# Mask rows of the last batch by compute engines, a fifth head pair by the crossbar, more buffers and a new instruction order in an attention and FFN kernel

## The chip, the cores and the metric

The kernel runs on one core of one Trainium2 chip. The metric is the device time of one execution in microseconds, as the median of the runs of a kernel. The engines are called TensorE (PE in the profile; its weight loads stand apart as PEld), VectorE (DVE), ScalarE (ACT), GpSimd (POOL) and SyncE (SP). A letter q behind an engine's name (SPq) means its instruction queue issuing a DMA.

## The reference, cut to what matters

Block-sparse attention over 4 batches of 8 heads, then a feed-forward block with a gated convolution along the sequence:

```python
def _attn_ref(q, k, v, sampled_blocks):          # B, H, S, D = 4, 8, 768, 64; blocks of 32
    scores = scale * np.matmul(q, k.transpose(0, 1, 3, 2))
    mask = np.abs(blk_i - blk_j) <= 1
    mask = mask | (blk_i == 0) | (blk_j == 0) | (blk_i == n_blocks - 1) | (blk_j == n_blocks - 1)
    for qb in range(n_blocks):
        for kb in sampled_blocks[qb]:
            mask[qb * 32:(qb + 1) * 32, kb * 32:(kb + 1) * 32] = True
    scores = np.where(mask, scores, -1000000000.0)
    attn = np.exp(scores - np.max(scores, axis=-1, keepdims=True))
    return np.matmul(attn / np.sum(attn, axis=-1, keepdims=True), v)

def _moe_ref(x, w_in, conv_w, w_out):            # x: 4 x 768 x 512, d_ff 1024
    h = np.maximum(x @ w_in, 0.0)
    conv_out = sum(conv_w[k] * hp[:, k:k + S, :] for k in range(3))   # hp: h padded by one
    gate = 1.0 / (1.0 + np.exp(-conv_out))
    return h * gate @ w_out
```

## The kernel before, in words

All 16 pairs of heads (P0 to P15, four pairs to a batch) are computed densely, with the mask as extra rows of the matrix product. For each pair the kernel holds two tiles, `e` and `o`, with 88 partitions: rows 0 to 63 hold transposed K and Q, one head dimension to a row, and rows 64 to 87 hold mask rows, one for each of the 24 blocks, which add a large negative number to the scores that are masked out. There are five such slots; the mask rows of a slot are written once, and serve every pair that comes to lie in the slot. In the last batch the queries of the second half of the sequence are grouped in another way (a segment of 256 tokens and one of 128 instead of one of 384), so the mask rows for these query columns have to be replaced in the slots of P12 to P15. The new rows stand ready in the tile `mlast`; before the change eight DMAs on SP's queue, called `m_last`, bring them into the slots (line 598).

Attention runs in 144 units. A unit is a set of score matmuls into PSUM (`s`, L746, two halves of four blocks), one exp on ScalarE over 128x1024 (L757), and eight matmuls with V (`av`, L779). Units 36 to 71 belong to batch 1; its pair P4 is needed from unit 36, P5 from 40.5, P6 from 45 and P7 from 49.5 on. VectorE divides by the sum (`rcp`, `norm`, L696 and L698), and the result is transposed into `xT`, mostly by DMA transposes on SP's queue (`x_xb`, L707). Between the units the feed-forward work of the segment before is done: `f1` (L895) and a relu on ScalarE or VectorE (L915, L917), for the convolution three `mul` (L949) and two `add` (L959) on VectorE, a tanh on ScalarE (L998), `g1` and `g2` on VectorE (L1001, L1006), and then `f2` (L825) with an eviction (`ev`) and an output DMA. `f2#3` needs the gates `g2#3` of the last pair of features in its first segment.

K, Q and V are loaded by GpSimd's queue (L240), which casts them to bf16 in `nat`, `nq` and `vn`. Pairs P0 to P4 (`NPE = 5`) get K and Q transposed by TensorE (`kq_transposes`: L470 for K, L508 for Q, the second half of Q from an `nq` buffer) and copied from PSUM. Pairs from P5 on go through the crossbar (`kq_crossbar`): two DMA transposes on SP's queue from `nat` to `stg` (L585, called `xb`), and two copies of 64x1536 from `stg` to the slot (`stg_cp`), both of which need both transposes. The loads up to batch 1 are issued in the order of `SEQ`, each after the load four places ahead of it has landed (L660, `pace`); later ones wait for the exp of a given unit (L417).

The whole order is fixed beforehand. Each operation has a place in `gr.ops`; `put_down` walks the string `ORDER`, in which two letters name an operation, one more the engine where there is a choice, and one more the buffer of each allocation. Every engine then executes its own instructions strictly in that order, and so does each DMA queue issue. The costs beside each operation, such as `t_d4`, `t_act` and the `service` of a DMA, were used to make the string and have no part in the execution. At the start 44 dummy matmuls (`NWARM`) and later 21 more (`NFILL`) keep TensorE busy.

Of the kernel before, what the change touches and what calls it, by code (L numbers as in the profile page):

```python
# [20 lines left out]
000b1e0010x020y030407080a0905060c0e0gV0d0WV10hA0UA0oA0f0B0z0i0XV0mV0VV0lV0nV0t0v1f1c01q11s21t1801E21G31m11Hr41
r5r6r7r8r9rarbrcrdrerfrgrhrirjrkrlrmrnrorprqrrrsrtrurvrw0Y00ZA012113A14ArxryrzrArBrCrDrErFrGrHrIrJ4n04o0+A0jA
0u0/04p00A10V11VrKrL4s115116A17A4t1g14x04y1j04u10p1hV11kV0q4z21lArM0rNrOrPrQrRrS4C14DrTrUrVrWrXrYrZr+4H0r/4I
1dV0s04q14r4v1iV0C1rV10r0s4E3s1s2s34Q14R4w4A4B4J44S5s44V04W4F1u04X04+14/1x14G530545011vV24K4L04T1zV1yV5c15d0E1
4U5521wV4M04N0F1FV25e34Y5h05i4Z1I01JV35m15n51521L15j45o51MV1NV1KV0D5r05s56575w15x5t05y11915f15g5F05G1n05k5l5K1
5L5p5q5u0N0J1aV5811bV1S00O0P0Q0R461A0470S481O1490T4a1U14b1V4c2414d2604e274f2c24g2e2591TV34h2f4i2k04j2m34k5H2
5M35v5P05Q5R41pV1oV5z4O15A05U15V5I4PV00I5B25C5J5N5O5W5610625a05S5T5X5Y630661675bV5Z05+5D15EV641656b06c5/060V
6811B11DV1CV6g16h6d26i3ht0hu6l0hq1hrhsV0hvAhO06m6t1hz06u6n46v5hw1hxhAhyAhPhQhBVhRhW16y06z696a6A06D16EhS6F1hT
hF06e1P1hG6fhYhHV6I06j6JhX6k6o6Q16R6q11QV6p06whI06xhJ1RVhZhUh+6r6K26S3hKA6V06WhL16+16/hM6X4705h/0w6s125V4hV0
hC0hDhNVhEVia26B6C6G730747816H6L6M6T1796U6Y1W16Z1Z07507a1i23ib6N21XV46O280296P1/A7g07h7i27l17m717276777n37b7c0  # L30
7q07r7s47j7k7v17w7o7pi0i4i31+Vi51YV7d0i6i1ic7e7x57D07E7t7F07uio07y7z7I17J7N0ii17G17Oijip7Hi77K12g12h7f7A1id7B
i8iei92aV07P27C2bVif7L7S17Tiq7M7Q7R7X07Yik7U37Z42n4l2s14m2u2002v1ig2dV0ih0k2lV1831847Vil88089ir8558a08d18e7W7+
7/0868i08j2iV12tV2imV02jVisV18020K818f18k2iu1iv8q18rix0iyiwA2o02pizViS0iUiT2qV22rViV8s38v08w8x487iD18A18B8C5
iA0iB8F0iE8b8c8G8g8K18h8L2x2w2C2y1822iCAiFA8H02F2G02D28M1i+1iWiXiM0iN8l8S08m2118TiOVi/8U2iP08X18t18Y8u8y8z8D
8Z322Vj0j18n023V8oiQiRA9008E8I8J91iG195196iHiJ0iK8N924975j2iYje3iZj3iIVjf8P1iLV8Qj629d09e8O08V8W8+9i19j9f08/93
9498999n09o9g19hj8j4j79a2j9j5ja9bjhjgji9k19p39s19tjs19x09y9u59z09l9m9qjE09F19r9G9v9K09LjFjb2I2H2Q2N2R22T2O09H2
8p2z2J08R2K9cjjjt9w9A9B09I9J9P19Qjcjdjkjl2AV39M1jujG9R49U09V9N9W3jva019Oa1jHjwA2a50a69Sa25jK19TjL9X9Y2LV42EV3
2MVjIV32BV9C09Da70aa1jN0abjOjMA1a31af0jT1agjUac2jPVk60jVV0Mk8k70Gk9ak1ala4jQ0ah4am32/2S3032Y2Z13231373829E0in
2U0itjJ2Va8jRas0atjSAjW1ax1aya9au1jXjZ0adj+az5jYAj/A2PV4kake19Z19+9/km2knkokpkfkqkbkckhaC0aDaeaiaH1aE0k31aIaj
kgkd1ank4k5Aap2jy0jzaP0aQk01ao0jAavawaAaBaJ2aR4aU1jBaVaZ0k1a+aFkrjCA0aW3a/1aGaKaLjm0b21b3jnb45kik2VaM0ku3aNkj  # L40
kvkwkxb70job8aS0bf1aTaXjpaYkI1bgb90bk0b0b1b5jqA1kkaqklkskyjx33134aOarbh2ktkzkC0kJblkDbm4bp1kKb6bqbabu0bvbb1
2+V02WV02XVkAkBkE35V1bc13a3b13f3cbr3bw1kLkFbibC1bDbH0bIbd39V1kGV336VkMA2kO1kR0kPkSbE5bJ0kTAbM1bNbjbR0bSbnbobs
btkU0bO2bxbykVbW1bXkQVla0lclbbT4kWAbY3bz0ldbAlelfkX1bF0kYc20bGbKbLkZVli1c3c71c8bPl10k+1l2c453d3e3m3p3q03u3n03r
3s3tlglkljl3Vllc91cc0cdce0bQk/ch1cibUl70bVbZcp0b+1l8cqc5l0Vlmcj2lnl41cu1cvcr4cw3c6cal5cz0cAcbcfcgckcE1cFclcB5
cG1be1kHjr3g03hlq2b/2lrlslolhltc0lul9Vcm1l6Vlpcnly3lzlAlBlvlClwlxcs0ctcxcJ0lM0cKlG1cycR1cScClNcDcHcL2cT4cW0cX
cY33E3B3F23J3G3H3C13I3Q3R2lHcIcMcN1c/1d0cUcVcZd40d5lOc+lIlD3v1bBc1cod10d65dc1ddde1cO0lElF3oV2cPlPd2lJdh0di0H
lKV33iV23jVlQA1dj2d3dm1dnm20d7do4m51d8m6dr0m33wd923xV3m4V0m7Adsdw1dxmq0mrdamtms3DV3dt3dy03T3U33Y3V3W3X43440me1
df0dgmh0dkmfmidE0dFdJ1mgAmjAm81dKm9mb0mcdG5maAdL1mu3yVmdVmy1mG2mvmHmAmwmzmBdO0dldpdqdudvdzdPdB1dT1mn1mk0mldA1
dUdHdQ2lRkNlL3K0cQ23L3Z1jD3+dbmmAdV4d/0modImpAlS0e0e13mCmO33MV4mImQdCmJlTe41e5lUlVe60mDmEmKmx0mFlY1lWA13SA4lZ
e90eaeb5l+ee1efdMdNdRdSdWdXe20dY0mPdZe3n00e7ej0e8mLeg1ekl/n1er1m0A2mR45V0mMmS0LmN3/V0el23ldDd+413AmTmUmV3NVec  # L50
edehmW1eiesmXew0exmYn2et4ey3eB1eCeD0mZn3emeG0eHeO1en1ePn4V340Veo2epm+A0nc1nf0ndngeI5eQ1nhAneVnC0nDnEnFnGeT0eU
eueY1evn61eZezeAn7eV2f10f2e+4f33nHn8Vn90eEeFnanbVnu1eJeKf61f7fe0ffeR0eSnl1nmeWnwnveL1nnVnxf80fg5fj1fkfl1eXni0
fo0fpfq2lX3k423O3Peq03ze/njno1ft1f0f4f5fuf9fB0fCnpnInynznkVnJnK2eMnLnr0fa1nsfhfinAfb0nMfcnqVnBnNfv4fD3fG1fHfm
fL0fnfMfrfsfwfxfE0fFntAfI0fy2nOfznS3nTnUnVnWfN5fT1fUfV1o40fJfY0fZn+1o5g11g2fKn/fOfPfW1fXnPf+2g34nXeNm/fdn5fAnQ
nRf/g0g90gag4ge1gfg5gb3o0o6nYnZgg0gj0o7fQ1o8V1g60fRo1gkgr1gsom0ono2A0g7ooV1op1oqgl5orAgc0gdoK0oMgt1os0ghgigw0
gxgmgnotov1owgB1gCgu1go2gpoLoNoOgy2ouAoxAgD4fS1oS1gqg8oH0gK0oIgLoB1oCgvgzgAgEoJAoE0gP1gQgM3oPoFgFgR0oToDVoUoV
oQgG1oWgHoGAp62p7oy1ozoAAo+3p8o/p9gX0gYh31gN0h4gOgZ5gSgT1og0ohgI1h80h9oiojg+g/h51gJAha2pq1prokA3oXgU2pap0h00gV
oR1h1p1oYpsApC0p2pbhh1pt0puhipw1pxpvApyApDoZo9o3gW2m1h2h60h7hbhc1pz0pAoa1pFhd1pcp3hep4pEobocodp5pdpGpBAhj4pK1
pS3p+2oeA1pk0plhkhlhf1hgApmpnq0hm2pLhnpUpoA0pHpMpTpNpIpVpOp/pJpWpe1pfpgho0phhpApiA2ql0qmqnAqr1qsqz0qi0qjqAqtA
qJ1qKqo1qppPqkApppjofolqB0qqApQq1pRq2pXqL1q3qCpYpZq60qu0qvqw3q4q5qMqNqxqyqc1qdq7qE1qFq8qG2qeqfqgA0qhq9qaA2qbqH  # L60
# [53 lines left out]
def kernel(  # L114
# [123 lines left out]
    def dma(name, eng, dst, src, prio, deps=(), service=0.3, kind="hw", **kw):  # L238
        occ = {"SP": 0.46, "ACT": 0.1, "POOL": SW}[eng]
        return op(name, {eng: occ}, lambda e: on(e).dma_start(out=dst(), in_=src), prio, deps,  # L240
                  dma=(kind, service), **kw)
# [84 lines left out]
    def dcopy(e, dst, src):  # L326
        if e == "ACT":
            nc.scalar.copy(out=dst, in_=src)  # L328
        else:
            nc.vector.tensor_copy(out=dst, in_=src)  # L330
# [739 lines left out]
```

## Time and profile before

| | before |
|---|---|
| runs, us | 206.09, 206.13, 208.36 |
| median, us | 206.13 |
| the profiled execution, us | 207.49 |
| its span, first to last instruction, us | 205.7 |
| granted clock of TensorE, mean | 0.999 |
| moved by DMA, MB | 25.96 |

The profile is of one execution, and all rows come from it; its time is 1.8 us above its span and 1.4 us above the median. In the busy table a number in brackets is the share of the span. In rows of groups the columns are the line, engine, operation, the tiles written and read, the shapes and the count, then total time, mean ns of one, and idle time of the engine ahead of it. In rows in order of time the columns are start and duration in microseconds, and a bracket at the end tells how long the engine had stood idle and what released it. Matmuls overlap one another, so a row's duration holds some 0.2 us of pipeline behind the last one.

### The profile page before, as it was taken

What the parts mean: (1) busy time and instruction counts of PE and PEld (TensorE: products, weight loads), DVE (VectorE), ACT (ScalarE), POOL (GpSimd) and SP (SyncE); (2) the same over time, 40 slices, a digit from 0 to 9 for tenths busy, and PEclk for the clock granted to TensorE, in tenths of its full rate; (3) what the DMA queues carried; (4) which work ended last, traced back from release to release, by engine and by line L of the source; (5) the groups of instructions that cost most, each with busy time, mean ns of one, the idle gap of its engine ahead of it and who ended that gap; (6) DMA issues with size and microseconds to landing.
All of it is one profiled execution on the core that took longest, in us unless ns stands there. A gap on an engine that the chain in (4) does not pass through costs nothing.

```text
span 205.7 us, 6845 instructions
## 1 busy us (share of the span) xinstructions
PE 197.3 (96%) x2698; PEld 154.4 (75%) x2716; DVE 180.3 (88%) x570; ACT 190.3 (93%) x252; POOL 57.9 (28%) x112
## 2 busy tenths in 40 slices
...
DMA  6999999999798983999997999993210401310523
GB/s 147 173 208 208 185 138 117 147 151 189 97 150 96 156 116 35 208 201 192 93 186 88 119 134 225 118 208 72 75 28 3 146 17 29 115 51 17 202 76 133
DMA packets 53655, 25.96 MB, mean 126 GB/s; under 512 B 39616, under 2 KB 50584, under 8 KB 53624
## 3 DMA queue, kind: packets, MB, share of 16 engines
...
q14 instruction: 10, 0.08, 0.2%
...
## 4 chain that ended last, share of the span: by engine, by line
PE 57%; ACT 16%; DMA 11%; DVE 10%; issue 3%; POOL 0%; ACTq 0%; DVEq 0%
PE st L746 18%; PE mix L895 14%; PE mix L825 13%; ACT pt L757 12%; PE av L779 10%; DMA stg<-nat 6%; DMA nat<-in_k_dram 3%; DVE m L949 3%; DVE m L959 2%; DVE hE L917 2%; DMA o2s<-in_q_dram 1%; PE mix L810 1%; ACT o L328 1%; ACT m L998 1%; DVE xtok L698 1%
## 5 line engine op out<-in xcount | busy, mean ns | idle before, releaser
L757 ACT ACTIVATE pt<-st 128x1024 bf16<-128x1024 f32 x144 | 140.0, 1034 | 2.8 <-PE st L746 2.1
L779 PEld LDWEIGHTS <-pt 128*128 128x128 bf16 x1152 | 51.8, 97 | 9.8
L779 PE MATMUL av<-vt,pt 128*128 128x65 bf16 x1152 | 59.1, 193 | 0.1
L895 PE MATMUL mix<-xT,winb 128*128 128x384 bf16 (+2 forms) x288 | 55.0, 308 | 0.5 <-DVE o2s L330 0.2
L949 DVE TENSOR_SCALAR m<-hE,cw 128x382 bf16<-128x382 bf16 (+2 forms) x192 | 49.0, 314 | 0.6 <-ACT hE L915 0.3
L825 PE MATMUL mix<-woutb,gT 128*128 128x512 bf16 x159 | 43.9, 379 | 1.3 <-DVE gT L1006 0.7
L746 PE MATMUL st<-o 88*128 88x128 bf16 (+1 forms) x240 | 44.4, 229 | 0.2
L746 PE MATMUL st<-o,e 88*128 88x128 bf16 (+1 forms) x228 | 43.4, 233 | 0.4 <-DVE o L330 0.3
L746 PE MATMUL st<-e 88*128 88x128 bf16 (+1 forms) x208 | 41.6, 239 | 0.8 <-ACT pt L757 0.2
L746 PE MATMUL st<-e,o 88*128 88x128 bf16 (+1 forms) x224 | 42.2, 234 | 0.1
L746 PEld LDWEIGHTS <-e 88*128 88x128 bf16 x436 | 33.5, 97 | 10.4 <-issue 1.7
L746 PEld LDWEIGHTS <-o 88*128 88x128 bf16 x464 | 34.9, 97 | 7.8 <-issue 0.9
L959 DVE TENSOR_TENSOR m<-m 128x764 bf16<-128x764 bf16 (+2 forms) x64 | 34.0, 532 | 0.3
L895 PEld LDWEIGHTS <-winb 128*128 128x128 bf16 x288 | 23.2, 97 | 6.6 <-issue 1.1
L998 ACT ACTIVATE m<-m 128x764 bf16<-128x764 bf16 (+2 forms) x32 | 26.4, 826 | 0.2 <-DVE m L959 0.2
L825 PEld LDWEIGHTS <-gT 128*128 128x128 bf16 x184 | 15.7, 97 | 9.6 <-DVE gT L1006 0.8
L417 POOL COPY pace<-pt 1x1 bf16<-1x1 bf16 x24 | 6.4, 267 | 51.3 <-ACT pt L757 51.2
L917 DVE TENSOR_SCALAR hE<-mix 128x384 bf16<-128x384 f32 x28 | 15.4, 554 | 4.0 <-PE mix L895 3.6
L915 ACT ACTIVATE hE<-mix 128x384 bf16<-128x384 f32 (+2 forms) x36 | 17.5, 505 | 1.2 <-PE mix L895 1.0
L1006 DVE TENSOR_TENSOR gT<-m,hE 128x764 bf16<-128x764 bf16 (+3 forms) x36 | 18.1, 510 | 0.4
L698 DVE TENSOR_TENSOR xtok<-av,rcp 128x384 bf16<-128x384 f32 (+2 forms) x36 | 18.1, 506 | 0.4
L240 POOL DMA_DIRECT2D nat<-in_q_dram x23 | 16.8, 733 | 2.7 <-issue 2.5
...
## 6 DMA issues: line engine op xcount, KB each, us to landing
...
```

Of the source, the lines that this page charges most:

```text
L698: nm = op("norm", {"DVE": t_dps(128 * C)}, lambda e: nc.vector.tensor_tensor(out=xtok_t[xk.index][:, 0:C].rearrange("p c h d -> p h c d"), ...
L746: nc.tensor.matmul(out=st[:, 128 * x:128 * (x + n_)], lhsT=QK[kc % 2][s][0:88, 1, hh, kc // 2, :], rhs=QK[par][s][0:88, 0, hh, idx:idx + n ...
L757: nc.scalar.activation(out=pt_t[ptb.index], in_=st_t[stb.index], func=AF.Exp, bias=0.0, scale=0.125)
L779: nc.tensor.matmul(out=o[:, off:off + 65], lhsT=pt_t[ptb.index][:, 128 * x:128 * x + 128], rhs=V_t[vslot_b[P].index][:, hh, kc, 0:65], sta ...
L825: nc.tensor.matmul(out=acc(), lhsT=gT_t[gb.index][:, ffc, 128 * t:128 * t + 128], rhs=woutb[:, ffc, :], start=(ffc == 0), stop=(ffc == NFF ...
L895: nc.tensor.matmul(out=mix_t[hb.index][:, w1 * y:w1 * y + w1], lhsT=winb[:, fc, 128 * ffc:128 * ffc + 128], rhs=xT_t[xt_buf[n].index][:, f ...
L915: i = nc.scalar.activation(out=dst, in_=src, func=AF.Relu, bias=0.0, scale=0.5)
L917: i = nc.vector.tensor_scalar(out=dst, in0=src, scalar1=0.5, scalar2=0.0, op0=ALU.mult, op1=ALU.max)
L949: i = nc.vector.tensor_scalar(out=m_t[cb.index][:, x, y, 0:w], in0=hE_t[heb.index][:, f0 + y, t0 + x:t0 + x + w], scalar1=cw[:, x, f0 + y: ...
L959: nc.vector.tensor_tensor(out=m[:, a_, :, 0:w], in0=m[:, a_, :, 0:w], in1=m[:, b_, :, 0:w], op=ALU.add)
L998: th = [op("tanh", {"ACT": t_act(2 * w) + 0.04}, lambda e, cb=cb, w=w: nc.scalar.activation(out=m_t[cb.index][:, 0, :, 0:w], in_=m_t[cb.in ...
L1006: i = nc.vector.tensor_tensor(out=gT_t[gtb.index][:, f0:f0 + 2, t0:t1], in0=m_t[cb.index][:, 0, :, 0:w], in1=hE_t[heb.index][:, f0:f0 + 2, ...
```

## The change

Five things change together.

1. The mask rows of the last batch: the eight `m_last` become copies by VectorE or ScalarE. In the new order seven are on VectorE (four of 24x512, three of 24x256) and one on ScalarE (24x256).
2. `NPE` goes from 5 to 4: P4 goes through the crossbar. Its 14 transposes on TensorE and six copies go; two DMA transposes and two `stg_cp` come. Its Q is loaded as one DMA of 192 KB instead of two of 96 KB, the second of which was the last of `SEQ`.
3. One more buffer for `stg` (2 to 3), `nat` (4 to 5), `vn` (3 to 4), `xtok`, `xT`, `m` and `o2s`, two more for `pt` (6 to 8).
4. One warm matmul and four fill matmuls less.
5. A new `ORDER`. The calls are the same otherwise; of the operations that may go to either engine some change sides (VectorE has one V copy and two output evictions more, and one relu less).

```diff
-    NF, NPE = 4, 5
+    NF, NPE = 4, 4
-    SEQ = "nq0 nq1 w0 w1 nq2 w2 nq3 w3 k4 q4 v4 k5 q5 v5 k6 q6 v6 k7 q7 v7 nq4"
+    SEQ = "nq0 nq1 w0 w1 nq2 w2 nq3 w3 k4 q4 v4 k5 q5 v5 k6 q6 v6 k7 q7 v7"
...
-    NSLOT, NSTG, NNAT, NVN, NPT, NXK, NXT, NHE, NCV, NGT, NOS = 5, 2, 4, 3, 6, 3, 3, 2, 4, 2, 4
+    NSLOT, NSTG, NNAT, NVN, NPT, NXK, NXT, NHE, NCV, NGT, NOS = 5, 3, 5, 4, 8, 4, 4, 2, 5, 2, 5
...
-    NWARM = 44
-    NFILL = 21
+    NWARM = 43
+    NFILL = 17
...
             for t, at, x0, n_ in ((O_t, 0, 1, 2), (E_t, 2, 2, 1)):
-                mr.append(dma("m_last", "SP", lambda t=t, x0=x0, n_=n_: t[slot.index][64:88, 0, :, x0:x0 + n_],
-                              mlast[64:88, at:at + n_].unsqueeze(1).broadcast_to([NB, 2, n_, 128]), due + 12, [o_ml],
-                              service=0.05, uses=[slot]))
+                mr.append(op("m_last", {"DVE": t_d4(256 * n_) + 0.05, "ACT": t_act(256 * n_)}, lambda e, t=t, at=at, x0=x0, n_=n_: dcopy(
+                    e, t[slot.index][64:88, 0, :, x0:x0 + n_], mlast[64:88, at:at + n_].unsqueeze(1).broadcast_to(
+                        [NB, 2, n_, 128])), due + 12, [o_ml], uses=[slot]))
```

`ORDER`, read letter by letter, in the stretch of batch 1's loads (xb and stg with the pair that they serve):

```
SP before:   x_xb#0, xb P5 k, xb P5 q, x_xb#1, xb P6 k, xb P6 q, x_xb#2, x_xb#3, xb P7 k, xb P7 q
SP after:    xb P4 k, xb P4 q, xb P5 k, x_xb#0, xb P5 q, xb P6 k, xb P6 q, x_xb#1, x_xb#2, x_xb#3, xb P7 k, xb P7 q

DVE before:  g2#2, stg P5 (2), g1#3, v_cp P5, g2#3, m_l, v_cp P6, stg P6 (1), v_cp P7, ev#0, stg P6 (2), ev#1
DVE after:   g2#2, stg P5 (2), stg P6 (1), g1#3, g2#3, v_cp P5, m_l, ev#0, v_cp P6, ev#1, v_cp P7, stg P6 (2)

PE before:   f2#2, s#82, s#83, av#78, f2#3, s#84, s#85, f2#7     (s#82 and s#83 are unit 41)
PE after:    f2#2, s#82, s#83, f2#3, s#84, s#85, f2#7
```

The copies of P4 (`stg` P4) stand on VectorE ahead of all of this. The `nq` buffer that the third pair's second Q load goes into is emptied by TensorE after s#27 before, and after s#29 in the new order. In the last batch SP's list has P14 k, x_xb#16, P15 k, an output, P15 q, P14 q, where it had P14 k, x_xb#16, P14 q, P15 k, an output, P15 q; in the first phase the casts and copies ahead of the first exp change between VectorE and ScalarE.

More of the change, by code (lines that the diff above doesn't have):

```diff
@@ L20 @@
 ORDER = """
[L21 to L60, printed above, removed]
@@ new lines @@
+521oV1pV1bV1TV31aV0Q0R401A0410S421O1430T441U4451V461+0472034821492614a2804b294c2e24d2g14e2h4f2m35A65i5j5n5o5I0
+5J5F75K05s5t04H15N15O5B5C5G5H0C5u25v0J0D4IV05P15W05X5L5M5w05Q5R5xV5Y25S35T5/16053154V6405Z1655U05+1B16135VV1CV
+1DV6646916ahj0hk6e06f6b56g6hm1hnhlV00NhoVhH0hJhI6m16n6o7hp06r06shs1ht6t06w16x6y1huVhKhq6B06Chv1hwhrVhLhP16D20w
+0v1W01XhxA6J1621P06K6367686O0hy1hz6P6c6d6h6i0hM6L3hQ1RVhRhShAVhT6j01QV6khX2hYhN6Q46T16UhE1hF6V5hU6Y06phB06Z6+6
+hC6q71172hDA7376u6v7907a6z6A6E6FhZhO0h+1YV46G2h/1ZV6HhV1/V46M16N6R6S7e17b06W7f6X6/707j07khGA7g1747507c7d761i33
@@ new lines @@
+7l27o17p7q3ib07h7i7w07m7x7n7r7shWi577i47B17Cih1iii07y42216l1237t3i1i67ui7i224V025V7G07H7D57I6ic7L17M7z17A7E7F
+7Jij7K7Q07Rid2a22b6I78i82cV1i9ia27V00k7v7N77S07Y17Zie810827+1832ifV02fV1ik861877OilV12nV22dV0Kin08b08cioiq1ir
+8838d42o2p22r2q2w2x02i02jipA8j18k7P8o07T8piw07U07/808l5isViL4iMiN8q68t18u8v784ix8y08z8A0iyAit1iu85892kV22lV7V0
+iOivV7WiT0iPiU8D18E8L08M8F18N28a8e8fiI1iF0iJiG8m18n8Q18R8r8s8V08WiKAiQiz18wiA8S38X48+18/905iV8g2iWiHViRiXj718h
+iBViS8x8B8CiC0iD960978G8H08O8PiEVj8iY8T9b19cjl18U9869g09h8Y8Z91929d78I1i/2j0iZ8Ji+j2j1933j394j9jajb9i19l19m9n3
@@ new lines @@
+9919a9q09rjx09e9s5j4j5j69f9y19j9z9kjm9A69D09ojy9p9t9E9u09B9I19J9Cjzjn2z2A42K2C2B2H2I12L32Njc9F02s17X28i2t8K2D2
+959K29N09Ojdje0H9v00M2uV3jo9G9P72yV3jpA2jA9V19WjBV39+09/9HjG1jHjD0jE9X1a04jFA19wjIV2vVj/3a31a4jM1a80a99LjNjJ0
+jKa53aa5jLAad1ae9M9Q9Ral0amk1k0jOVk29S2k74af6jP19Y1jS0an2jTjQk8k99Tk3jUAjRAkf0kakbaq1arav09Za1awjV0a2jWa6a7jY1
+as7k4khkgki2Ekj2FV4ax4jZaA1aBabacagjXAj+Akc2JV4kdai1ah0aoapjf0aI0aJataujr1jgaC5aK22V2M2W02Y2S2T22XaN1aOjsaS0ay
+aTjtazaDaP0aX1aY9x32O02Z12P2+jCkn2ajk5kok612GVkpimak9UjujvV4jqaU1aZ3kkaEaL1aMaQaRaVb00b1jhb81b9kv1b270GaF3klke
@@ new lines @@
+kqaGaHjwjibd0bekwba4jjA3krkmksbi1aWa+kB0bf5313233435139363738bjkxkCa/bn0bokDbk6bp22/V02QV1kt2RVkub3bv1bwb50ky
+kE30VkFV1b6bx0bA0bBb40bF1bGkzA22UV0kK1kH0bC1kLbK0bLbH3kMVkIkJVl31l4l5l6l733V1bM7bbbP1bQbckQ1bgbX0bYbhblkRkN0bm
+kObqbR4bZ5kSAkPAc01brby1c1bzkT1bDkUc50c6kW0bEbs1lb3lcbtldl8c26leca1cbc70cc1kVVlfl9lgkXbIbJbNbOci0kYVbSbT0cjla
+lj4lkkZ1llcn1cob+l00l1b/c3c4ck3cs0ctcp4l2Ak+lmlhbU2k/VbVcx1c8c9cylz0cdcelr0lncf3licglsltlucu63j3g3k23o3h03l3m
+3ncz2cC0cDcE7jk3a2b703p03b3qbubWchlocl1cmlF1cqcK1crcLcP0cM5lAcQcvcwcAcBlGcU1cFcG0cVcR1lvlpcH0lqcNcZ0c+cOcScTlH
@@ new lines @@
+lBlwcW3d51cXd6c/4lx3cV2ly3rV3cIlIlCd72lDA4lJV3da0cYdbd0d1d81lX1df1dgdc5dh3lYdk0dll+03v3w13y3z43D3A3B3N3C3K3L2
+3O33S3P3Q3Rdm0l/3tV3iV20Ld213xV33eVlZV0m0Vdp1dqdr63Z3+3m41m5m10m2dx0m6AdydC1ma1dDmbm3A3sVmj2d3mkmmmr1mtms3dVml
+mnmudz7mcAm70dH0dE4dIm8m9Amz3md1med9dM1dNdddedJ1mfAdO2mg0mhdU0didVdjlR1dndodW5miVdZ1d+lL0e20e3lMd/3mvmAmB3MV4
+mCkG3E1cJ13T0lE3U3FkAdsdt0dAdBdFdu2mDdGdKmH4mJdve40momwmElNdLdPe71dQe8lSlTec0edlOdX1dYe0lUigd4dwdR3mpmImxmKmq0
+dSmLmydT3GV4mFmG3VV13fVe963JAlPA1ek1e1e5ele6mV0ee7em4lVA4mMep0eqmWeu1eveaew1mP1ebmQmNmO3/V03HVefeg0mRez1eAer2
@@ new lines @@
+eB5mS3uV3WVmXmYeH0eI3YVmZV2eh0ei3IVmTA0eJ3eM1eNenn51eO0n80n9naVn6n7Anv0nwnxnyeR0eSeW1eT6eXeom/0n21n0n3eY7n1A
+n4Vnznn2e/0f0esetexf71f8f14nAne0nb1eyfc0eCeDnfeK1fdncf92ngAfe1npnonBeE1nqeFndVnrnCnD1eLePeQfh1eUfieVnk0nleZe+
+fj5nsfm0fnf2nh1fu1fvnif30fafbnEf42nGnmVnFf5ntnjVnufo3fw0fz0fAfffgfkflfE1fFfpfqfx1fyfB6fM0fNfr3nL3nNfsnHnMnOnP
+ej2mUlWlKf6eGftfG7fO4nT0fR1fSfT2nIfCfDfHnZ1fIfW0fP0fQfXn+fY1nQg21g3nUfUfVfZg70g8nJnKfJ0nVf+n/g45nRnSfK3XVg93
+gc1o0o1V0nWgdg51g6gagk0f/2nXV4ge0of1ogoi0ojg0ohV1gbglgfoo1ggopokVoD4ol0omoFoEgh1gm6oqAonAgp1gqoGgioL0oMgr7ox1
```

12 lines of the change are left out of this document (11 added, 1 removed).

## The prediction

> **What bounds the kernel now.** I read the page first, then the busy time by stretches, then the chain of waits, then single waits in time order.
>
> ```profile
> span 205.7 us, 6845 instructions
> ...
> PE 197.3 (96%) x2698; PEld 154.4 (75%) x2716; DVE 180.3 (88%) x570; ACT 190.3 (93%) x252; POOL 57.9 (28%) x112
> ...
> DMA  6999999999798983999997999993210401310523
> ...
> PE 57%; ACT 16%; DMA 11%; DVE 10%; issue 3%; POOL 0%; ACTq 0%; DVEq 0%
> ...
> L757 ACT ACTIVATE pt<-st 128x1024 bf16<-128x1024 f32 x144 | 140.0, 1034 | 2.8 <-PE st L746 2.1
> ```
>
> TensorE carries the kernel (57% of the chain of waits, 96% busy). DMA has 11% of the chain, and its slices read 9 over most of the first 28 of 40. So a change of order can win only what TensorE now loses, and that loss is concentrated:
>
> ```profile
> core 0: us, PE busy (x) PEld busy (x) DVE busy (x) ACT busy (x) POOL busy (x), PEclk, DMA share, GB/s
> 30.00:35.00 5.00, 5.00 (x81) 4.18 (x79) 4.99 (x18) 4.97 (x8) 3.67 (x8) 1.00 0.95 122
> 45.00:50.00 5.00, 4.78 (x63) 3.30 (x63) 3.76 (x10) 4.96 (x6) 0.00 (x0) 1.00 1.62 158
> 50.00:55.00 5.00, 4.45 (x55) 3.37 (x56) 4.16 (x12) 4.39 (x5) 2.56 (x5) 1.00 1.19 130
> 120.00:150.00 30.00, 29.11 (x356) 21.29 (x357) 26.46 (x77) 29.05 (x39) 6.91 (x13) 1.00 0.93 134
> ```
>
> At 45 to 55 TensorE, VectorE and ScalarE are all below full while the DMA share is highest: the batch-1 loads. The chain names what they wait for:
>
> ```profile
> 39.01 6.53 DMA nat<-in_k_dram
> ...
> 45.56 7.25 DMA stg<-nat
> ```
>
> P6's second crossbar transpose was issued at 45.56 and landed 7.25 us later, at 52.81. On the engines:
>
> ```profile
> 49.05 0.55 DVE L330 COPY e<-stg 64x1536 bf16<-64x1536 bf16 x1 [1.21 <-DMA stg<-nat]
> ...
> 50.22 0.36 DVE L1001 TENSOR_SCALAR m<-m 128x764 bf16<-128x764 bf16 x1
> ...
> 50.76 0.55 DVE L1006 TENSOR_TENSOR gT<-m,hE 128x764 bf16<-128x764 bf16 x1
> ...
> 51.37 0.61 PE L825 MATMUL mix<-woutb,gT 128*128 128x512 bf16 x2
> ...
> 52.91 0.55 DVE L330 COPY e<-stg 64x1536 bf16<-64x1536 bf16 x1 [0.71 <-DMA stg<-nat]
> ```
>
> VectorE, in order, stood 1.21 us for P5's data and 0.71 us for P6's. Between them it did g1 (50.22) and g2 (50.76), on which f2#3 at 51.37 rests. TensorE lost a little more behind it, in weight loads of f1:
>
> ```profile
> 54.48 0.42 PEld L895 LDWEIGHTS <-winb 128*128 128x128 bf16 x3 [0.37 <-issue]
> ...
> 55.88 0.42 PEld L895 LDWEIGHTS <-winb 128*128 128x128 bf16 x3 [0.28 <-issue]
> ```
>
> The second loss is where the last batch comes in:
>
> ```profile
> 136.52 0.55 DVE L330 COPY e<-stg 64x1536 bf16<-64x1536 bf16 x1 [1.06 <-DMA stg<-nat]
> ...
> 140.18 0.39 PE L825 MATMUL mix<-woutb,gT 128*128 128x512 bf16 x1 [0.67 <-DVE gT L1006]
> ```
>
> VectorE waits 1.06 us for a transpose, so a gate is late, and TensorE waits 0.67 us for it.
>
> **Fewer warm and fill matmuls, and the start: nothing.** In the first phase TensorE waits for ScalarE, so five dummies less only leave a longer wait:
>
> ```profile
> 11.74 0.22 PE L746 MATMUL st<-e 88*128 88x128 bf16 x1 [0.19 <-ACT pt L757]
> ```
>
> The casts and copies ahead of the first exp change engine one for one; I keep that at zero.
>
> **The fifth pair (P4) by the crossbar.** TensorE loses 14 transposes:
>
> ```profile
> 39.35 0.50 PE L470 MATMUL mix<-ident,nat 128*128 128x128 bf16 x6
> ```
>
> Six take 0.50 us with the 0.22 us of a single one at the end, so (0.50 - 0.22) / 5 = 0.056 us each and 0.78 us in all. Ten of the 14 lie before 51.37, where DMA sets the time, and are worth nothing. The four of the second half came later: **-0.2 us**. P4's copies change from 64x768 and smaller to two of 64x1536; the prices are near each other, and VectorE waited 1.21 us there anyway: zero.
>
> ```profile
> L330 DVE COPY e<-stg 64x1536 bf16<-64x1536 bf16 x11 | 5.9, 548 | 3.0 <-DMA stg<-nat 3.0
> L330 DVE COPY e<-mix 64x768 bf16<-64x768 bf16 x4 | 2.2, 539 | 1.5 <-PE mix L470 1.5
> ```
>
> In exchange SP issues two more transposes, ahead of those of P5 and P6:
>
> ```profile
> 9.26 1.48 SPq L361 DMA_DIRECT2D o<-o  x2
> 36.59 1.30 SPq L707 DMA_TRANSPOSE xT<-xtok  x1
> ...
> 41.23 1.33 SPq L707 DMA_TRANSPOSE xT<-xtok  x1
> ...
> L585 SPq DMA_TRANSPOSE stg<-nat x22: 1209/1254/3088, 38.0 to 135.2; - x22
> ```
>
> On SP's queue they cost nothing: it issued nothing between 10.74 and 36.59, and P4's data, which TensorE took at 39.35, is loaded in that time. On the DMA engines two transposes at the median of 1.254 us are 2.5 us at most, and nothing if the DMA engines have room. In 30 to 35, where they will run, the DMA share is 0.95 against 1.62 later, so I take a quarter: +0.6 us.
>
> **The order of batch 1, the step that decides.** The new order puts P6's first copy on VectorE right behind P5's two, before the g1 and g2 of the last feature pair. What is queued behind that wait: g1#3, g2#3, three V copies, two evictions. Who waits for these: f2#3, which stands in TensorE's list before the scores of unit 42, so the whole of TensorE. When does P6 land? From 52.81: the transpose that stood at 41.23 now comes after P6's, -1.33; P4's, +0.6; sum 52.1. Then copy 0.55, g1 0.36, g2 0.55: f2#3 at 53.5 instead of 51.37. The later losses of 0.37 and 0.28 then fall away, since what they waited for has arrived. So 53.5 - 51.37 - 0.65 = **+1.5 us**. The lower end is P6 landing with P5 and both waits gone, -(1.21 + 0.71) = -1.9. The upper end is 52.81 + 2.5 with nothing won on SP's queue, and 1.0 more because the load chain starts one exp later (L757, 1.034 us) in the new order:
>
> ```profile
> 20.43 0.72 POOL L240 DMA_DIRECT2D nq<-in_q_dram  x1 [5.63 <-PE mix L508]
> ```
>
> That load waits until TensorE has emptied an nq buffer, and the new order puts that transpose one exp later. 56.3 + 1.46 - 51.37 - 0.65 = +5.8.
>
> **More buffers.** The fourth vn buffer removes this wait:
>
> ```profile
> 11.00 0.74 POOL L240 DMA_DIRECT2D vn<-in_v_dram  x1 [1.32 <-DVE vt L330]
> ```
>
> Late next is the load at 20.43, which waits for TensorE all the same: zero. The third stg buffer lets P7's transposes go before P5 is copied; P7 is needed 4.5 units after P6, so zero too.
>
> **The mask rows.** Eight DMAs leave SP's queue, seven copies come to VectorE and one to ScalarE:
>
> ```profile
> L240 SPq DMA_DIRECT2D e<-mlast  x4: 779/779/899, 138.7 to 148.0; - x4
> L240 SPq DMA_DIRECT2D o<-mlast  x4: 815/828/994, 142.9 to 150.1; - x4
> ...
> L330 DVE COPY e<-e 24x384 bf16<-24x384 bf16 x2 | 0.7, 380 | 0.0
> L328 ACT COPY o<-o 24x384 bf16<-24x384 bf16 x1 | 0.5, 507 | 0.0
> ```
>
> SP is freed of 4 x 0.779 + 4 x 0.828 = 6.4 us. They started at 138.7, after the transpose that VectorE waited for at 136.52, so their removal alone does not cure that wait. What does is the new place of P14's and P15's transposes with a third stg buffer; the wait of 1.06 us then goes, **-1.1 us** (bounds -1.1 and 0). On VectorE the seven cost 7 x 0.38 = 2.7 us; ScalarE's one is 0.5 us. VectorE's idle time in 120 to 150 is 30 - 26.46 = 3.5 us, of which 1.1 has been spent; 2.4 remain to hide 2.7, so I take **+0.3** (bounds 0 and 2.7). If that cover is gone, the copies delay the gates and so f2.
>
> **Sum.** -0.2 + 1.5 - 1.1 + 0.3 = +0.5 us on the profiled execution, which took 207.49 us (span 205.7 and 1.8 around it): 208.0. The three runs have a median of 206.13, 1.36 below it; on the median the same sum gives **206.6 us**. A measurement of this kernel tells about 2% from no change, that is 202.0 and 210.3.
>
> **Rivals.**
>
> *Faster.* P6 lands with P5 and both waits go: -0.2 - 1.9 - 1.1 + 0 = -3.2, 202.9 us. For it: SP's queue stands empty before 36.59, and transposes issued early meet a smaller share. Against it: all slices from 2 to 9 read 9 for DMA.
>
> *Slower.* P6's copy blocks VectorE to the end. The new transposes come out of the same DMA time as the loads of P5 to P7. At the upper end, -0.2 + 5.8 - 1.1 + 0.3 = +4.8, 210.9 us. It decides once P6 lands after 55.7: then this step costs over 5.1 and the sum passes 4.1, which is 2%. For it: a share of 1.62 and 7.25 us for one landing. Against it: the share of 0.95 before 35. The Trainium skill speaks for it in "DMA: Bandwidth & Descriptors", section "Issuing engines are not separate DMA queues": DMAs from the sync, scalar and gpsimd engines run on the same 16 engines and interleave, and another issuing engine saves only issue time. By that rule the two transposes are paid in full, and the trace agrees as far as the 7.25 us at the share of 1.62 go.
>
> *VectorE becomes the bound in the last batch.* All 2.7 us of copies show and the wait of 1.06 stays: -0.2 + 1.5 + 2.7 = +4.0, 210.1 us. For it: 88% busy. Against it: ScalarE and TensorE are fuller there (29.05 and 29.11 of 30).
>
> That the mask DMAs were hidden anyway is no rival of its own; without the -1.1 the time is 207.7.
>
> **Chances.** My forecast 0.46 (its own range 204.7 to 208.7, about half way to the rivals on each side); the faster rival 0.16, of which 0.07 lies under 202.0; P6 blocking 0.26, of which 0.16 lies over 210.3; VectorE 0.12, of which 0.06 lies over it. So faster by over 2% 0.07, slower 0.16 + 0.06 = 0.22, within 0.71. The range from 202.9 to 210.9 has the two outer rivals' own times as its ends; half of each, 0.08 and 0.13, lies beyond.
>
> **What would show it.** VectorE's wait ahead of P6's first copy, which I expect at 52.1 less the end of P5's copies near 50.2, about 2 us: under 0.5 us is the faster rival, over 5 us the slower one. f2#3 at 53.5. No wait over 0.3 us on a stg copy after 120, and VectorE over 28.5 of 30 us busy there. P4's transposes issued before 36. I am wrong if the start shifts by over 0.5 us, or if TensorE loses time in batch 2, where I priced nothing.

## The result, and the profile after

The changed kernel takes 216.22 us (median of 6 runs, 214.75 to 217.23), the kernel before 207.91 us beside it (6 runs, 206.09 to 208.92). The ratio is 1.0406, with a 95% interval of 1.0339 to 1.0473: slower by about 8.4 us, where I had forecast 206.6 us and put the upper end of the range at 210.9.

The page of the profile after (the profiled execution took 217.23 us), with the span, the busy times, the slices of granted clock and DMA, and the chain of waits:

```profile
span 215.4 us, 6771 instructions
...
PE 200.6 (93%) x2676; PEld 157.2 (73%) x2697; DVE 182.0 (84%) x578; ACT 189.0 (88%) x249; POOL 55.9 (26%) x110
...
PEclk9999999957859999999999999999999999999999
DMA  6999999999976839899496999996122116103213
...
PE 44%; DMA 19%; DVE 13%; ACT 12%; issue 7%; SPq 2%; POOL 2%; POOLq 0%; ACTq 0%; DVEq 0%
```

The span grew by 9.7 us. TensorE's part of the chain fell from 57 to 44%, that of DMA rose from 11 to 19%. The granted clock, which is 1.00 in every stretch shown of before, falls to half in two of the slices between 43 and 65 us. Busy times by stretches show where the loss lies (columns as in the rows shown of before; the DMA share adds up the times of all packets over 16 engines, and passes 1 where they overlap):

```profile
30.00:35.00 5.00, 5.00 (x70) 3.98 (x69) 4.94 (x17) 5.00 (x7) 4.08 (x9) 1.00 1.18 142
35.00:40.00 5.00, 4.81 (x88) 4.09 (x85) 4.40 (x14) 5.00 (x8) 1.25 (x3) 1.00 1.58 135
40.00:45.00 5.00, 1.73 (x40) 1.59 (x37) 2.08 (x5) 3.04 (x4) 2.88 (x6) 0.91 1.86 129
45.00:50.00 5.00, 4.61 (x52) 3.94 (x53) 3.13 (x13) 2.45 (x3) 0.87 (x2) 0.50 1.52 83
50.00:55.00 5.00, 4.95 (x56) 3.47 (x56) 3.22 (x8) 4.05 (x6) 0.00 (x0) 0.91 1.46 158
55.00:60.00 5.00, 1.32 (x9) 0.64 (x8) 2.10 (x7) 1.80 (x2) 0.89 (x2) 0.78 1.51 131
60.00:65.00 5.00, 5.00 (x31) 3.36 (x30) 3.05 (x9) 2.34 (x3) 1.21 (x2) 0.54 0.83 148
```

TensorE is busy 1.73 of 5 us at 40 to 45 and 1.32 of 5 at 55 to 60. In between it looks busy, but at 45 to 50 the clock is 0.50, and matmuls take longer at such a clock: the two of f2#3 last 1.04 us at 59.30, where they lasted 0.61 before. The exp of unit 60 starts at 83.60 us, before at 74.27: 9.3 us lost. From there to the end of the span both kernels need nearly the same, 131.8 and 131.4 us.

The rows in order of time that end these two holes, by VectorE and TensorE:

```profile
42.85 0.55 DVE L330 COPY e<-stg 64x1536 bf16<-64x1536 bf16 x1 [3.45 <-DMA stg<-nat]
45.17 0.82 PE L779 MATMUL av<-vt,pt 128*128 128x65 bf16 x12 [3.44 <-DVE xtok L698]
57.83 0.55 DVE L330 COPY e<-stg 64x1536 bf16<-64x1536 bf16 x1 [4.58 <-DMA stg<-nat]
59.30 1.04 PE L825 MATMUL mix<-woutb,gT 128*128 128x512 bf16 x2 [3.68 <-DVE gT L1006]
```

The first copy is P4's: VectorE stands 3.45 us for the crossbar, and the division by the sum queued behind it makes TensorE wait 3.44 us. The second is P6's first copy, placed ahead of g1#3 and g2#3: VectorE stands 4.58 us, and f2#3 starts at 59.30. And the chain of waits says why P6 came so late:

```profile
35.95 12.15 DMA nat<-in_q_dram
48.15 9.66 DMA stg<-nat
```

P6's Q load was issued when it was before (35.95 and 35.96 us), but its data was there only 12.15 us later, where before it had landed by 41.18 us, and the transpose that followed took 9.66 us, against 7.25 before.

### The profile page after: what moved, and what is told of

Same layout as the page of the kernel before. It is cut to its first block, busy times and chain, and to the rows that moved or that the text cites. A ratio compares the mean times of both kernels' runs of the same rounds, so it can differ in the third digit from the quotient of the medians.

```text
span 215.4 us, 6771 instructions
## 1 busy us (share of the span) xinstructions
PE 200.6 (93%) x2676; PEld 157.2 (73%) x2697; DVE 182.0 (84%) x578; ACT 189.0 (88%) x249; POOL 55.9 (26%) x110
## 4 chain that ended last, share of the span: by engine, by line
PE 44%; DMA 19%; DVE 13%; ACT 12%; issue 7%; SPq 2%; POOL 2%; POOLq 0%; ACTq 0%; DVEq 0%
PE st L746 12%; PE mix L895 11%; PE mix L825 11%; ACT pt L757 8%; PE av L779 6%; DMA nat<-in_q_dram 6%; DMA stg<-nat 4%; DVE m L949 4%; DMA xT<-xtok 3%; DMA woutb<-in_moe_w_out_dram 3%; PE st L1027 2%; DMA nat<-in_k_dram 2%; DVE m L959 2%; DVE hE L917 1%; PE mix L810 1%
## 5 line engine op out<-in xcount | busy, mean ns | idle before, releaser
L779 PEld LDWEIGHTS <-pt 128*128 128x128 bf16 x1152 | 52.6, 98 | 14.0 <-issue 4.1
L895 PE MATMUL mix<-xT,winb 128*128 128x384 bf16 (+2 forms) x288 | 53.6, 309 | 0.8 <-DMA xT<-xtok 0.7
L825 PE MATMUL mix<-woutb,gT 128*128 128x512 bf16 x156 | 45.7, 388 | 4.5 <-DVE gT L1006 3.7
L746 PE MATMUL st<-o 88*128 88x128 bf16 (+1 forms) x240 | 46.2, 233 | 0.1
L746 PE MATMUL st<-e,o 88*128 88x128 bf16 (+1 forms) x224 | 44.2, 240 | 0.5 <-ACT pt L757 0.4
L746 PE MATMUL st<-o,e 88*128 88x128 bf16 (+1 forms) x228 | 44.2, 235 | 0.2 <-ACT pt L757 0.2
L746 PEld LDWEIGHTS <-o 88*128 88x128 bf16 x464 | 36.2, 100 | 9.1 <-issue 1.9
L895 PEld LDWEIGHTS <-winb 128*128 128x128 bf16 x288 | 24.0, 98 | 8.8 <-issue 1.4
L417 POOL COPY pace<-pt 1x1 bf16<-1x1 bf16 x24 | 5.1, 212 | 56.9 <-ACT pt L757 56.7
L240 POOL DMA_DIRECT2D nat<-in_q_dram x23 | 17.6, 769 | 3.2 <-issue 2.9
```

The source lines that it names most:

```text
L746: nc.tensor.matmul(out=st[:, 128 * x:128 * (x + n_)], lhsT=QK[kc % 2][s][0:88, 1, hh, kc // 2, :], rhs=QK[par][s][0:88, 0, hh, idx:idx + n ...
L779: nc.tensor.matmul(out=o[:, off:off + 65], lhsT=pt_t[ptb.index][:, 128 * x:128 * x + 128], rhs=V_t[vslot_b[P].index][:, hh, kc, 0:65], sta ...
L825: nc.tensor.matmul(out=acc(), lhsT=gT_t[gb.index][:, ffc, 128 * t:128 * t + 128], rhs=woutb[:, ffc, :], start=(ffc == 0), stop=(ffc == NFF ...
L895: nc.tensor.matmul(out=mix_t[hb.index][:, w1 * y:w1 * y + w1], lhsT=winb[:, fc, 128 * ffc:128 * ffc + 128], rhs=xT_t[xt_buf[n].index][:, f ...
```

## The experiments

The theory before the runs (D in the expectations): P4's two transposes share the DMA engines with the loads of P5 to P7, everything lands later, and what waits for it stands in VectorE's list ahead of work that TensorE needs. Against it stood that the list alone costs (W), that the lowered clock costs, that the mask copies cost, and that the new order costs without any crossbar. Ratios are to the kernel before on the same chip; the last two columns are the start of P6's first copy on VectorE and VectorE's wait ahead of it.

| kernel | us | ratio and interval | P6's copy, us | wait, us |
|---|---|---|---|---|
| after | 216.22 | 1.0406 (1.0339 to 1.0473) | 57.83 | 4.58 |
| after, copies of P4 and P6 late | 213.15 | 1.0205 (1.0129 to 1.0281) | 56.69 | 0 |
| after, only P4's late | 215.99 | 1.0407 (1.0356 to 1.0459) | 56.88 | 5.14 |
| after, only P6's late | 211.52 | 1.0191 (1.0126 to 1.0256) | 56.03 | 1.49 |
| after, dummy matmuls in the stalls | 216.48 | 1.0343 (1.0261 to 1.0426) | 58.81 | 6.25 |
| after, mask rows by DMA | 215.01 | 1.0266 (1.0176 to 1.0356) | 55.52 | |
| after, loads held | 215.81 | 1.0443 (1.0326 to 1.056) | 56.12 | 2.62 |
| after, P4 by TensorE, P6's copy early | 209.64 | 1.0085 (1.0035 to 1.0135) | 51.70 | 1.12 |
| after, P4 by TensorE, P6's copy late | 208.67 | 1.0111 (1.0045 to 1.0178) | 53.73 | 0 |
| before, P4 by the crossbar | 208.45 | 1.0099 (1.0048 to 1.015) | 55.31 | 1.35 |
| before, two transposes nobody reads | 209.74 | 1.0162 (1.0092 to 1.0232) | 55.22 | 2.26 |
| before, four transposes nobody reads | 214.86 | 1.0321 (1.0251 to 1.0392) | 58.53 | 0 |
| before and the mask copies | 208.76 | 1.0019 (0.9977 to 1.006) | | |

### VectorE's list

Only the order of VectorE is edited (`norm` is the division by the sum; a number in brackets tells how many of a pair's two copies stand there):

```diff
 VectorE, first run (both), second (P4 alone), third (P6 alone)
-mul#8, g2#0, add#4, stg P4 (1), rcp#5, add#5, stg P4 (1), norm#5, ... norm#6, mul#10
+mul#8, g2#0, add#4, rcp#5, add#5, norm#5, ... norm#6, stg P4 (2), mul#10           # both; P4 alone
-g2#2, stg P5 (2), stg P6 (1), g1#3, g2#3, v_cp P5, m_l, ev#0, v_cp P6, ev#1, v_cp P7, stg P6 (1)
+g2#2, stg P5 (2), g1#3, g2#3, v_cp P5, m_l, ev#0, v_cp P6, ev#1, v_cp P7, stg P6 (2)  # both; P6 alone
```

> Only VectorE's list changes: P4's two copies from stg move behind the normalisations of the same stretch, P6's first copy moves behind the gates, V copies and evictions that stood behind it. Theory W (late data become TensorE stalls because these copies stand too early on VectorE, and each stall over 3 us halves the clock): TensorE's two stalls of 3.4 and 3.7 us fall below 1.5 us together, the granted clock stays at 1.00 between 40 and 65, and the time is 207 to 210 us against 216.2. Theory D (the data are late because P4's transposes and the loads share the DMA engines, and the pairs are needed soon anyway): P6 still lands near 57, the scores of unit 45 wait for it, and the time is 212 to 215 us.

> After, with pair 4's two copies alone moved behind the work of pair 2 on VectorE (pair 6's first copy stays early). Theory B (both early copies cost, pair 4's about half of the 3 to 4 us that moving both brought): 213 to 215 us, ratio 1.025 to 1.035, VectorE's wait for pair 6 still about 4 us. Rival P (pair 4's wait costs all of it): as with both moved, 212 to 213.5 us. Rival Q (pair 6's costs all): 215.5 to 217.

> After, with pair 6's first copy alone moved to just before its second (pair 4's copies stay early). Theory B: 213 to 215 us, and the stall at 42 to 47 us stays at 3 us or more. Rival P: 215.5 to 217. Rival Q: 212 to 213.5.

Both late: 213.15 us. P4 late alone: 215.99, nothing won. P6 late alone: 211.52, all of it. So rival Q holds (the last time lies 0.5 us under its range), and my theory that both share the cost falls. The rows in order of time, with P4's copies alone late:

```profile
44.15 0.54 DVE L330 COPY e<-stg 64x1536 bf16<-64x1536 bf16 x1
...
56.88 0.55 DVE L330 COPY e<-stg 64x1536 bf16<-64x1536 bf16 x1 [5.14 <-DMA stg<-nat]
58.35 1.04 PE L825 MATMUL mix<-woutb,gT 128*128 128x512 bf16 x2 [5.32 <-DVE gT L1006]
```

P4's copy waits for nothing now, and the exp of unit 36 starts at 46.44 us instead of 49.31. But P6 still lands only at 56.88, 1 us earlier than in after; VectorE waits 5.14 us there instead of 4.58, and TensorE 5.32 behind it: what was won ahead of the arrival is waited away at the arrival. With P6's copy alone late, P4's wait remains, though shorter, and the rows are:

```profile
40.87 0.55 DVE L330 COPY e<-stg 64x1536 bf16<-64x1536 bf16 x1 [1.67 <-DMA stg<-nat]
43.22 0.52 PE L779 MATMUL av<-vt,pt 128*128 128x65 bf16 x12 [1.59 <-DVE xtok L698]
...
56.03 0.55 DVE L330 COPY e<-stg 64x1536 bf16<-64x1536 bf16 x1 [1.49 <-DMA stg<-nat]
56.45 0.32 PE L895 MATMUL mix<-xT,winb 128*128 128x384 bf16 x1 [2.42 <-DMA xT<-xtok]
```

f2#3 no longer appears as a wait. What is left at 56 us is the next thing that DMA brings late, an `xT` transpose, which SP issues behind P6's.

### The clock

50 and 60 dummy matmuls are put on TensorE ahead of the two matmuls that waited:

```diff
 after, TensorE
+50 x matmul(st, warm, warm)      # ahead of av#62
+60 x matmul(st, warm, warm)      # ahead of f2#3
```

> All waits stay; 50 dummy matmuls (2.8 us) go into TensorE's first stall and 60 (3.4 us) into the second, into score banks that are free then. Theory G (part of the loss is the halved clock after each stall): the granted clock stays at 1.00, VectorE still waits 3.4 and 4.6 us for stg, and the time falls by 3 to 5 us to 211 to 213. If DMA alone sets the time in this stretch, the clock is restored and the time stays at 215 to 217.

The time is 216.48 us, as if DMA alone set it. The stretches:

```profile
45.00:50.00 5.00, 4.36 (x72) 3.44 (x70) 4.97 (x18) 3.17 (x4) 1.40 (x3) 1.00 1.49 97
55.00:60.00 5.00, 2.57 (x46) 2.39 (x43) 1.15 (x3) 0.00 (x0) 0.30 (x1) 1.00 1.18 142
60.00:65.00 5.00, 4.66 (x30) 3.25 (x32) 4.00 (x13) 2.20 (x3) 1.21 (x2) 0.66 0.80 134
```

The clock is 1.00 at 45 to 50 where it had been 0.50, and the exp of unit 36 comes 0.8 us earlier. P6's copy still starts only at 58.81, after a wait of 6.25 us, so what the clock gave in the first stall was waited away. In the second stall the clock was not kept up: TensorE still stood idle for 2.72 us behind the dummies, and 0.66 at 60 to 65 is little better than the 0.54 of after. What the lowered clock costs there is not shown; the ratio is 0.6% under that of after, and the intervals overlap.

### The mask rows

```diff
 after, last batch
-op("m_last", {"DVE": ..., "ACT": ...}, copy mlast into the slot)
+dma("m_last", "SP", the same rows)               # eight, at the places of before
```

> The mask rows of the last batch go back to eight DMAs on SP's queue; everything else stays. Theory M (the copies load VectorE in the last batch): 2 to 3 us faster, 213.5. Theories W and D: all is lost by unit 48, so 216 within 1 us; if the SP queue was what the change relieved, up to 1 us slower.

The median is 215.01 us. The profiled execution was the fastest of the four, 212.25 us, and in it P6 happened to land at 55.52. From the exp of unit 60 to the end it needs 131.8 us, as after does. So the copies give and take nothing in their own stretch; why the whole is lower by 1.2 us, which the two intervals do not separate, stays open. The other way round, in the kernel before:

```diff
 before, last batch
-dma("m_last", "SP", ...)                         # eight on SP
+op("m_last", {"DVE": ..., "ACT": ...}, copy)     # seven on VectorE, one on ScalarE
```

> The kernel before with the mask rows alone changed: seven copies on VectorE and one on ScalarE in place of the eight DMAs, at places next to those of after; all else as before. My forecast's step said -1.1 for the DMAs and +0.3 for the copies, so 205.5 to 207 us, ratio 0.993 to 0.998. Rival T (TensorE is the bound in the last batch, so neither shows): ratio 0.999 to 1.003.

1.0019 (0.9977 to 1.006): the copies by themselves have no effect that can be told, as rival T says. The expectation misread my prediction: there the -1.1 comes from the new place of P14's and P15's transposes and from the third `stg` buffer, and this run has neither. It tests the +0.3 alone, a ratio of 1.0015, and that lies within the interval.

### The crossbar alone, and the order alone

In after, `NPE` goes back to 5, with P6's copy where after has it; in a later run P4's TensorE work is placed two to three units later and P6's copy stands late. In before, `NPE` goes to 4, with P4's copies placed late:

```diff
 after                                    before
-NF, NPE = 4, 4                          -NF, NPE = 4, 5
+NF, NPE = 4, 5                          +NF, NPE = 4, 4
-SP: xb P4 k, xb P4 q                    +SP: xb P4 k, xb P4 q          # behind m_dma
-VectorE: stg P4 (2)                     +VectorE: stg P4 (2)           # behind norm#6
+TensorE: 14 transposes of P4            -TensorE: 14 transposes of P4
```

> P4 goes back to TensorE's transposes and PSUM copies, with its second half of Q loaded separately; the order of the other copies, with P6's first copy still early on VectorE, and all buffers stay. Theory D: without P4's two transposes the Q load of P6 lands in 5 to 7 us instead of 12.15, VectorE waits under 2 us for P6, and the time is 205 to 209 us. Theory W alone: VectorE still waits 3 to 5 us ahead of P6's first copy, TensorE stalls once by about 3 us and loses its clock once, and the time is 210 to 213 us.

> After with pair 4 by TensorE as before (its transposes and copies two to three exponentials later than in the earlier run of this kind, which had stalled 2.5 us at 40 to 45 us), and pair 6's first copy moved to just before its second. New order, late buffers and mask copies stay. Theory D: no stall over 1.5 us left between 33 and 60 us, 205 to 208 us, ratio 0.99 to 1.005. Rival R (the new order has a cost of its own): 209 us or more.

> The kernel before with one edit: pair 4 comes by the crossbar (14 transposes issued ahead of pair 5's), its two copies late on VectorE, behind the pair 3 work; order, buffers and mask rows as before. Theory D (pair 4's transposes share the DMA engines with the loads of pairs 5 to 7 and both slow down): pair 6's first copy at 54 to 59 us against 51 before, and 211 to 216 us, ratio 1.02 to 1.04. Rival R (the new order and the new buffer counts cost, the crossbar does not): 206 to 209 us, ratio under 1.01, pair 6's copy within 1 us of before's.

Without the crossbar the new order, with the new buffers, the mask copies and the fewer dummy matmuls, which no run separates, costs 0.9% with P6's copy early and 1.1% with it late. These two runs also differ in the place of P4's work. Their waits are those of theory D, but both times, 209.64 and 208.67 us, lie 0.6 to 0.7 us above its ranges. In the rows in order of time of the first, P6's early copy costs TensorE 0.86 us:

```profile
51.70 0.55 DVE L330 COPY e<-stg 64x1536 bf16<-64x1536 bf16 x1 [1.12 <-DMA stg<-nat]
53.17 0.60 PE L825 MATMUL mix<-woutb,gT 128*128 128x512 bf16 x2 [0.86 <-DVE gT L1006]
```

That is my forecast's picture, to the half microsecond (52.1 and 53.5), of a kernel without P4's transposes. The crossbar without the new order costs 1.0%: P6's copy, at 55.31, lies within theory D's range, but the cost is half of the least that it gave. Crossbar and order together, with P6's copy late, cost 1.9%, about their sum. So after's 4.1% is about 1% for the crossbar, 1% for the order, and 2% for what they do to each other (each ratio is known to some 0.5 to 0.7%): the crossbar makes P6 late, and the order puts all of TensorE behind P6.

The run with P4 by TensorE and P6 late also shows where the order's own 1% arises. Its exp of unit 60 starts at 74.35 us, level with before. Then, in batch 2:

```profile
78.31 1.18 SPq L707 DMA_TRANSPOSE xT<-xtok  x1
79.80 0.97 PE L895 MATMUL mix<-xT,winb 128*128 128x384 bf16 x5 [1.31 <-DMA xT<-xtok]
```

TensorE comes to an f1 before its `xT` has been transposed. From 65 to 120 us it is busy 53.27 us there, before 54.60; from 120 to 150 it makes up 0.5 us (29.60 against 29.11). Unlike the rest, this is read from the trace and was not tried with another order.

### Sharing the DMA engines, measured by itself

Two (then four) transposes of P4's K block go into a spare buffer that nobody reads, in the kernel before, where after issues P4's:

```diff
 before, SP
 m_dma#3
+dma_start_transpose(out=spare, in_=nat of P4, K)      # x2; in another run x4
 x_xb#0
```

> The kernel before, pair 4 still by TensorE, plus two crossbar DMAs that transpose pair 4's K block into a staging buffer that nobody reads, issued where after issues pair 4's. Nothing on any engine waits for them but SP's own queue and the DMA engines. Theory D: loads and later transposes slow by the sharing alone: pair 6's first copy at least 2.5 us later than before's, 210 to 215 us. Rival C (the cost is the engines' waits on pair 4's own data, not the sharing): 207 to 209 us, ratio under 1.01.

> The kernel before plus four crossbar DMAs that nobody reads in place of the earlier run's two, at the same place in SP's queue. Theory D (the DMA engines are at their limit from about 33 to 54 us, so each extra transpose delays all that is behind it): twice the cost, ratio 1.03 to 1.04, pair 6's first copy at 57 us or later. Rival S (a slack is used up once, or the first pair only met a lucky order): ratio 1.015 to 1.022.

No engine waits for these transposes, and yet two cost 1.62%, 3.4 us (0.0162 x 207.72; interval 1.9 to 4.8), and four 3.21%, 6.7 us (interval 5.2 to 8.1): twice as much. Two alone fall just short of theory D's marks (P6's copy 2.3 us later, not 2.5; 209.74 us, not 210), and rival C's ratio is passed; four meet theirs. The rows of VectorE's first copies of P5 and P6, with two and then with four:

```profile
49.81 0.55 DVE L328 COPY e<-stg 64x1536 bf16<-64x1536 bf16 x1 [1.92 <-DMA stg<-nat]
55.22 0.78 DVE L328 COPY e<-stg 64x1536 bf16<-64x1536 bf16 x1 [2.26 <-DMA stg<-nat]
```

```profile
55.47 0.55 DVE L328 COPY e<-stg 64x1536 bf16<-64x1536 bf16 x1 [4.28 <-DMA stg<-nat]
58.53 0.55 DVE L328 COPY e<-stg 64x1536 bf16<-64x1536 bf16 x1
```

P6 went from 52.91 to 55.22 and 58.53 us. With four, it is P5's copy on which VectorE stands 4.28 us, and since P5's copies are ahead of g1#3 in the order of before, TensorE waits 2.5 us for the gate there too: the same trap, one pair earlier.

The extra transposes stand on SP's queue, ahead of those of P5 and P6, so a delay in that queue alone would be a rival. The loads decide it, since GpSimd issues them on a queue of its own. These are the four that it issues between 31 and 37 us (Q and V of P5, K and Q of P6), in before, with two, with four, and in after, where P4's own two are on their way:

```profile
DMA to landing us min/median/max: 4.9/5.3/5.6
DMA to landing us min/median/max: 6.6/7.0/7.2
DMA to landing us min/median/max: 6.8/8.4/9.5
DMA to landing us min/median/max: 8.2/9.4/12.2
```

Loads of the same size, issued at nearly the same times by another engine, take longer with every transpose added.

Could the loads be kept out of the transposes' way instead?

```diff
 after, GpSimd
+hold: copy one element of P4's stg (waits until P4's transposes have landed)
 ld_k P5, ld_q P5, ld_v P5, ld_k P6, ...
```

> After, with one more instruction: GpSimd reads one element of pair 4's staging buffer before it issues pair 5's K load, so that the loads of pairs 5 to 7 start when pair 4's transposes have landed (about 5 us later than in after). Theory M (transposes and loads in flight together are slow, each alone is quick): pair 4 lands by 37 us instead of 42.8, pair 6's first copy by 55 against 57.8, and 208 to 213 us. Rival V (it is only the volume that the DMA engines have to move): everything of pairs 5 to 7 lands about 5 us later than in after, and 217 to 222 us.

GpSimd's row, and the first copies of P5 and P6:

```profile
36.42 0.28 POOL L588 COPY pace<-stg 1x1 bf16<-1x1 bf16 x1 [6.15 <-DMA stg<-nat]
...
52.36 0.55 DVE L328 COPY e<-stg 64x1536 bf16<-64x1536 bf16 x1 [6.01 <-DMA stg<-nat]
...
56.12 0.57 DVE L328 COPY e<-stg 64x1536 bf16<-64x1536 bf16 x1 [2.62 <-DMA stg<-nat]
```

P4 landed by 36.42 us and not at 42.8, as theory M wanted, and although the loads started 6 us later (K of P5 at 36.87 instead of 30.56), P6 came no later than in after (56.12 against 57.83). So running both at once won little here: what overlaps is slowed by about as much as it overlaps. But the time, 215.81 us, is no better, since VectorE now stands 6.01 us for P5. It lies between the ranges of M and V; what the mixing alone costs stays open.

## Why the prediction was wrong

**The step that decides failed in its size.** "The order of batch 1, the step that decides" named the right wait, the right queue behind it and the right instruction on TensorE; its price came from P6 landing at 52.1, at the latest at 56.3. It landed at 57.8, f2#3 started at 59.30 and not at 53.5, and the step of +1.5 (at most +5.8) became most of the 9.3 us lost at the exp of unit 60. VectorE's wait of 4.58 us in the profile stands just under the 5 us that I had named as the sign of the slower rival, and P6's 57.8 is past the 55.7 at which I had that rival decide. So its mechanism is what happened, in a dearer form than the 210.9 us that I gave it, and with the smaller chance. Put into my own sum, 57.8 makes the step +7.2 and the whole +6.2 us; some 2 us of the 8.3 measured are not in it, and stay open.

**The term under it was "P4's, +0.6".** I took a quarter of 2 x 1.254 us, because the DMA share before 35 us was 0.95. Two transposes that nobody waits for cost 3.4 us (1.9 to 4.8), over five times the term; four cost 6.7 us (5.2 to 8.1), where my bound of 2.5 us for two would make 5.0. Two things were overlooked. The duration at SP is that of issuing and not of the transfer, as the tile `stg` shows in after from 30 to 64 us (min, median and max, ns for the nine issues, and us to landing of those whose landing the profile tells):

```profile
L585 SPq DMA_TRANSPOSE stg<-nat x9: 1211/1876/2756, 31.0 to 62.0; - x9
...
DMA to landing us min/median/max: 5.1/7.1/12.2
```

And the share of 0.95 was that of the stretch in which they are issued, while the work that they push back has to pass at 40 to 60 us. The rule of the Trainium skill that I had set against it ("DMA: Bandwidth & Descriptors", section "Issuing engines are not separate DMA queues": they share the engines and interleave) is borne out by the cost doubling with their number.

**The -1.33 us on SP's queue** was not to be had either. In before, P6's Q had landed by 41.18 us, as the copy on GpSimd that waits for it shows, and P6's two transposes stood in SP's queue, behind an `x_xb`, until 42.66 and 45.56. (The chain's load at 39.01, which I read as what they wait for, is P7's K by the order of `SEQ`.) In after the same copy on GpSimd starts at 48.22, and P6's second transpose is issued at 48.15: the load held it, and no longer the queue. The two rows, of before and of after:

```profile
41.18 0.82 POOL L660 COPY pace<-nat 1x1 bf16<-1x1 bf16 x1 [0.47 <-DMA nat<-in_q_dram]
...
48.22 0.18 POOL L660 COPY pace<-nat 1x1 bf16<-1x1 bf16 x1 [3.25 <-DMA nat<-in_q_dram]
```

The 1.0 us at my upper end, for the load chain starting one exp later, did show (the load of 20.43 us stands at 21.43 in after), but was made up by P6's Q load.

**P4's copies, "zero".** In the trace they look like half of the loss, 3.45 us. Moving them won nothing as long as P6 was waited for, and nothing once it was not (1.0205 with both late, 1.0191 with P6's alone). Zero was right, though not for the reason I gave.

**The lowered clock** I had not priced. The dummies show that it did not set the time at the first stall; at the second they did not keep it up.

**The mask rows, -1.1 and +0.3.** Alone in the kernel before the copies give 1.0019 (0.9977 to 1.006), in which my +0.3 (1.0015) lies. No run tests the -1.1 alone. In after the wait on a stg copy after 120 did go, and the copies are cheaper than the 0.38 us I took, as the rows of the tile `mlast` show:

```profile
L330 DVE COPY o<-mlast x4: 284/284/288, 133.7 to 177.4; 24x512 bf16<-24x512 bf16 x4
...
L330 DVE COPY e<-mlast x3: 218/218/219, 153.7 to 156.8; 24x256 bf16<-24x256 bf16 x3
```

But a wait of VectorE is worth only what TensorE waits behind it. I had booked the 1.06 us of VectorE, and TensorE, busy 29.11 of 30 us, had waited 0.67 us for it. In the like stretch of after (130.8 to 160.8 us) it is busy 29.66 us, 0.55 more. VectorE as the bound of the last batch did not come: it is busy 28.14 us there, under the 28.5 that I had named.

**Batch 2**, where I priced nothing and said that a loss would prove me wrong, has one: the wait for `xT` in the new order, 1.31 us with P4 by TensorE and P6's copy late, and 0.69 us in after. **The start** shifted by 0.64 us at the first exp (7.36 against 6.72), over the 0.5 I had named, and was level again by the third (9.18 and 9.23); in other runs with the same start the first exp comes at 6.62 to 7.49. **The faster rival** was not in reach: no run brought P6 in with P5. None of the twelve variants was faster than the kernel before.
